# A two-branch layer: w1 blocks paired at a distance, and the rows that their pairing leaves unused no longer loaded

## The chip, the cores and the metric

The kernel runs on one core of a Trainium2 chip. The metric is the device time of one execution in microseconds (us). The kernel before takes 145.11 us, the median of three runs (144.78 to 145.85).

## The reference

The input x has 2048 tokens of D = 448 channels. It is normalised once, and two branches start from the normalised tokens. Both results and x itself are added.

```python
xn = layernorm(A_x)                                # (1, 2048, 448), no scale, no shift
q, k, v = split(xn @ A_wqkv)                       # 16 heads of 28
phi(t) = concat(softmax(t @ w_phi), softmax(-(t @ w_phi)))
o = phi(q) @ (phi(k)^T v) / (phi(q) . sum(phi(k)))  # linear attention
h = silu(xn @ B_w1)                                # 448 -> 1792
out = x + o @ A_wo + h @ B_w2                      # 1792 -> 448
```

Everything is in bf16 with f32 sums. The case is about `B_w1`, the 448 x 1792 matrix of the second branch.

## The kernel before

**The rows of w1.** 448 rows do not fill whole groups of 128 partitions. The kernel holds w1 as four row tiles (kt 0 to 3) that begin at rows 0, 128, 256 and 320 (`KS`). Tile 2 holds rows 256 to 383, tile 3 rows 320 to 447, so rows 320 to 383 are held twice: in the upper half (partitions 64 to 127) of tile 2 and in the lower half of tile 3. `w1_sb` is a view of the buffer `flat` (phT in the profile), 1792 columns per tile; the same buffer later takes the transposed phi(q).

**A pair of column blocks.** w1 has 14 column blocks of 128. `ffn1_block` (L783) multiplies two of them, i = 0 and 1, with 512 tokens, and hands the work to `pair_block` (L755). There block i = 0 uses tile 2 whole and the upper half of tile 3, block i = 1 uses tile 3 whole and the lower half of tile 2. That covers the 448 rows for each, and neither touches the doubled rows of its other tile. Two matmuls of 64 rows run beside each other in the two halves of the array. The pairs fp = 0 to 6 are blocks (0,1), (2,3) and so on. A third function, `evac`, writes Silu of both blocks from PSUM into hT (ScalarE, tile hT).

**The order of the work.** Every operation is recorded once, with its dependencies worked out from the memory that it reads and writes; a list scheduler sets each engine's order, and TensorE's is written out by hand in `PLAN`. Each operation then waits for semaphores of those it depends on. In `PLAN`, aFn and bFn are the first and second half of the matmuls of the n-th pair (n counts the pairs of the first 512 tokens, then those of the next), av and bv, ak and bk, aq and bq the same for two token tiles of v, k and q, f and g the folding of w_phi into wqkv, Y and G the second FFN product, W the output projection. It begins:

```python
PLAN = """r0 aF3@4 r2 r1 bF3 aF6@0 aF4@6 bF6 bF4 aF5@4 av2@2 av0@0 bv2 bF5 bv0 av4@6 aF10@2 ...
```

Before that stands a head in which F0, F1 and F2 (pairs 0, 1, 2 with the first 512 tokens) run token tile by token tile, as the tiles come out of the layernorm, interleaved with TensorE transposes; r0, r1, r2 are their last matmuls, those of the remaining half tiles.

**The loads.** `load` (L561) issues one DMA on SP's queue (three of x go by ScalarE's queue, four small ones by GpSimd's). In order, SP issues: x0; w1_0 (tiles 0 and 1 of columns 0 to 511) and w1_0r (tiles 2 and 3 of them); two loads for columns 512 to 767; x4 (tokens of tiles 4 to 7); two for 768 to 1023; two for 1024 to 1791; two for wv; x8 and x12. `load_rows4` is a load of tiles 0 to 2 and one of tile 3. Behind the loads the same queue issues DMA transposes (`dma_t`, L632): wT_dma4 to 7 (columns of wqkv, for the fold; tiles wT and Y_sb), then xnT_dma5 and xnT_dma7 (the normalised tiles 4 and 5, 6 and 7; xnT<-RA), then wT_dma8 and, with waits for the layernorm, the further ones, then w2 and wo. av4 needs xnT_dma5, aF10 (pair 3 with tokens 512 to 1023) needs xnT_dma7 too, and the first fold, f0, needs wT_dma4 to 8.

Of the kernel before, what the change touches and what calls it, by code (L numbers as in the profile page):

```python
# [8 lines left out]
ACTF = mybir.ActivationFunctionType  # L9
# [361 lines left out]
def bass_parallel_sum__linear_kernel_hedgehog__dense_activation_silu__prompt_kernel(  # L371
# [10 lines left out]
    S, D, H, DH, FF = 2048, 448, 16, 28, 1792  # L382
# [18 lines left out]
    def rows_of(a, t0, t1):  # L401
        for u0, u1 in TILES:
            if u0 <= t0 < u1:
                v = a[0][128 * u0:128 * u1, :].rearrange("(p t) d -> p t d", p=128)
                return v[:, t0 - u0:t1 - u0, :]
# [3 lines left out]
    with es:  # L409
        def sb(name, shape, dt):  # L410
            return es.enter_context(nc.sbuf_tensor(name, shape, dt))
# [26 lines left out]
        hT = sb("hT", [128, FT, S], BF16)  # L438
# [3 lines left out]
        flat = phT[:]  # L442
# [5 lines left out]
        w1_sb = flat[:, 0:4 * FF].rearrange("p (k f) -> p k f", k=4)  # L448
# [59 lines left out]
        def d_mm(n):  # L508
            return max(n * 0.4167 + 2.5, 40.0)

        def d_act(n):
            return n / 1.2 + 60.0
# [7 lines left out]
        def pe_mms(mms, name, dur=None, keys_w=(), mode=128):  # L520
            def fn(e):
                r = None
                for dst, lhsT, rhs, st, sp in mms:
                    r = e.matmul(dst, lhsT, rhs, start=st, stop=sp, skip_group_check=True)  # L524
                return r
            n = 1
            for _, cnt in mms[0][2].ap[1:]:
                n *= cnt
            o = P.op("pe", dur if dur is not None else d_mm(n), fn, reads=[m[1] for m in mms] + [m[2] for m in mms],
                     writes=[m[0] for m in mms], keys_w=keys_w, name=name, mode=mode)  # L530
            o.words = 2 * len(mms)
            return o

        def mm(dst, lhsT, rhs, st, sp, name, keys_w=()):
            pe_mms([(dst, lhsT, rhs, st, sp)], name, keys_w=keys_w)
# [10 lines left out]
        def act(dst, src, func, n, name, scale=1.0, table=None, **keys):  # L546
            P.op("act", d_act(n), lambda e: e.activation(dst, src, func, scale=scale),  # L547
                 reads=[src], writes=[dst], table=table, name=name, **keys)
# [8 lines left out]
        def load(dst, src, name, eng="sp", lat=1700.0):  # L557
            n = 2
            for _, cnt in list(dst.ap):
                n *= cnt  # L560
            P.dma(lambda e: e.dma_start(out=dst, in_=src), n / 280.0, writes=[dst], name=name, eng=eng, lat=lat)  # L561
# [35 lines left out]
        def load_x(t0, t1, eng="sp"):  # L597
            load(x_sb[:, t0:t1, :], rows_of(A_x, t0, t1), f"x{t0}", eng, lat=1400.0)

        def load_rows4(dst, src, c0, c1, name, eng="sp"):  # L600
            load(dst[:, 0:3, :], src[0:KF, c0:c1].rearrange("(k p) f -> p k f", p=128), name, eng)
            load(dst[:, 3, :], src[D - 128:D, c0:c1], name + "r")

        def load_w1(c0, c1, eng="sp"):
            load_rows4(w1_sb[:, :, c0:c1], B_w1, c0, c1, f"w1_{c0}", eng)
# [3 lines left out]
        load_x(2, 3, "act")  # L609
        load_x(3, 4, "act")  # L610
        load(w1_sb[:, 0:2, 0:512], B_w1[0:256, 0:512].rearrange("(k p) f -> p k f", p=128), "w1_0")
        load(w1_sb[:, 2:4, 0:512], bass.AP(B_w1.tensor, B_w1.offset + 256 * FF, [[FF, 128], [64 * FF, 2], [1, 512]]), "w1_0r")
        load_w1(512, 768)
        load_x(4, 8)
        load_w1(768, 1024)
        load_w1(1024, FF)
        load_rows4(wv_sb, A_wqkv, 2 * D, 3 * D, "wv")
        load_x(8, 12)
        load_x(12, 16)
# [135 lines left out]
        def pair_block(b0, width, lhs, rhs, name):  # L755
            def part(c0, c1, steps=(0, 1, 2)):
                for i in range(2):
                    for n, kt in ((n, (0, 1, 2 + i)[n]) for n in steps):
                        mm(banks[b0 + i][:, c0:c1], lhs(i, kt, slice(0, 128)), rhs(i, kt, slice(0, 128), c0, c1),
                           n == 0 and c0 == 0, False, name)  # L760

            def rest():
                rows = [HIGH, LOW]
                return [(banks[b0 + i][:, 0:width], lhs(i, 3 - i, rows[i]), rhs(i, 3 - i, rows[i]), False, True) for i in range(2)]

            first = []

            def half(i):
                lo, hi = i, 1 - i
                mms = []  # L770
                for n, (kl, kh) in enumerate(((0, 0), (1, 1), (2, 3)) if i == 0 else ((0, 0), (1, 1), (2, 2), (3, 3))):
                    st, sp = i == 0 and n == 0, i == 1 and n == 3
                    mms.append((banks[b0 + lo][:, 0:width], lhs(lo, kl, LOW), rhs(lo, kl, LOW), st, sp))
                    mms.append((banks[b0 + hi][:, 0:width], lhs(hi, kh, HIGH), rhs(hi, kh, HIGH), st, sp))
                o = pe_mms(mms, name, dur=len(mms) // 2 * d_mm(width), mode=64)
                if i == 0:
                    first.append(o.id)
                else:
                    o.after = first[0]

            return part, rest, half

        def ffn1_block(fp, c, b0):  # L783
            tok = slice(c * 512, (c + 1) * 512)
            fns = pair_block(b0, 512, lambda i, kt, r: w1_sb[r, kt, (2 * fp + i) * 128:(2 * fp + i + 1) * 128],
                                    lambda i, kt, r, c0=0, c1=512: xnT_sb[r, kt, c * 4 + c0 // 128:c * 4 + c1 // 128, :], "ffn1")

            def evac():
                src = psum[:, b0 * 512:(b0 + 2) * 512].rearrange("p (b c) -> p b c", b=2)
                act(hT[:, 2 * fp:2 * fp + 2, tok], src, ACTF.Silu, 1024, "silu", table="silu", okeys_r=["acttab"])  # L790

            return *fns, evac

# [250 lines left out]
        def F(n, b0):  # L1044
            return ffn1_block(*chunk[n], b0)
# [3 lines left out]
        for word in "tr0a tr0 tr1 00a 10a 00b 10b 01a 11a 01b 11b 20 tr2 21 tr3 02a 12a 22a 02b 12b 22b 03 13 23".split():  # L1049
# [3 lines left out]
            f, t = int(word[0]), int(word[1])  # L1053
# [54 lines left out]
        for word in PLAN.split():  # L1108
            n0 = len(P.ops)
            kind, arg = word[0], word[1:]  # L1110
            if kind == "r":
                b, f = (0, 2, AUX)[int(arg)], head[int(arg)]
                pe_mms(f[1](), "rest", dur=d_mm(512), mode=64)
                f[3]()
            elif kind in "ab":
                turned = kind == "b"
                kind, (arg, _, at) = arg[0], arg[1:].partition("@")
                t = int(arg)
# [12 lines left out]
                elif kind in "GY":  # L1131
                    bs = pair_banks(t, at)
                    k = done.get((t, turned), 0)
# [27 lines left out]
            else:  # L1161
                assert kind == "E"
                t = int(arg)
# [114 lines left out]
```

## Time and profile before

| | |
|---|---|
| median of three runs | 145.11 us |
| the profiled execution | 144.51 us, its span 143.3 us |
| TensorE matmuls (PE) | 140.2 us busy, 98% of the span, granted clock 1.00 |
| VectorE, ScalarE, GpSimd | 90.2, 79.6, 75.2 us busy |
| read from HBM | 6.57 MB |
| loads of w1, as landed | 10.85 and 11.52 us for the last two, 6.3 or less from issue |

The span runs from the first instruction to the end of the last; the profiled execution's own time is 1.2 us more than that. PE counts as busy while a matmul is in its pipeline. Names such as psum<-xnT,phT say what an instruction writes and reads; an L number is a line of the kernel, and since helpers record the operations, all matmuls of the layer have line L524. SPq is the sequencer of SyncE, which issues DMAs; its durations are those of the issue, not of the transfer. A DMA lands when its last packet has been counted.

### The profile page before, as it was taken

The page shows a single profiled execution, that of the slowest core. Times are in us where ns is not written, and L with a number is a line of the kernel's source. Part 1 is how long each engine was busy: PE and PEld are TensorE (multiplying, and loading weights), DVE is VectorE, ACT ScalarE, POOL GpSimd, SP SyncE. Part 2 cuts the span into 40 slices and gives each one's busy share as a digit, 9 for nine tenths or more (in the row PEclk, how much of TensorE's full clock was granted, in tenths as well). Part 3 has the DMA queues.
Part 4 walks back from the last instruction along what each step waited for, and adds up shares of the span by engine and source line. Part 5 has one row for each costly group of instructions (what it writes and reads, how often), then busy time and mean ns, then how long its engine had stood idle before and what let it go on. Part 6 is the DMA issues. An engine that isn't in the chain of part 4 may idle for free.

```text
span 143.3 us, 4555 instructions
## 1 busy us (share of the span) xinstructions
PE 140.2 (98%) x1966; PEld 82.4 (58%) x1966; DVE 90.2 (63%) x194; ACT 79.6 (56%) x98; POOL 75.2 (53%) x95
## 2 busy tenths in 40 slices
PE   7999999999999999999999999999999999999994
PEld 7894444445444544476677655555555555555773
DVE  1988897600850079939049999957976564265533
ACT  4669676479996999888888948265440000000000
POOL 8828566620395009899935999992594800000000
DMA  4999989745990000000000068859589999825522
GB/s 133 354 318 380 165 168 84 158 81 93 344 300 7 0 2 5 0 0 5 0 5 5 5 116 162 129 109 164 97 159 134 230 225 159 143 48 105 167 91 64
DMA packets 45188, 17.59 MB, mean 123 GB/s; under 512 B 36960, under 2 KB 44784, under 8 KB 45168
## 3 DMA queue, kind: packets, MB, share of 16 engines
q1 hardware_dynamic: 42304, 15.14, 54.8%
q10 hardware_dynamic: 2736, 2.14, 5.1%
q8 instruction: 15, 0.25, 0.7%
q0 software_dynamic: 128, 0.03, 0.2%
q14 instruction: 5, 0.04, 0.1%
HBM read 6.57 MB, written 1.84 MB: 59 GB/s over the span
## 4 chain that ended last, share of the span: by engine, by line
PE 95%; DVE 2%; DMA 1%; ACT 0%; issue 0%
PE psum L524 94%; DMA x_sb<-in_A_x_dram 1%; DVE st L709 1%; PE psum L541 1%; DVE RA L724 0%; DVE mv L710 0%; DVE x_sb L1010 0%; ACT ve L713 0%; DVE rstd L715 0%
## 5 line engine op out<-in xcount | busy, mean ns | idle before, releaser
L524 PE MATMUL psum<-xnT,phT 64*128 64x512 bf16 (+1 forms) x428 | 46.8, 350 | 0.0
L524 PE MATMUL psum<-w_sb,hT 64*128 64x448 bf16 (+4 forms) x455 | 46.0, 341 | 0.0
L844 DVE TENSOR_REDUCE Rec<-Ek_sb 128x32 f32<-128x896 bf16 (+1 forms) x20 | 24.6, 1257 | 18.6 <-ACT Ek_sb L547 18.6
L524 PEld LDWEIGHTS psum<-w_sb,hT 64*128 64x128 bf16 (+1 forms) x455 | 23.6, 94 | 17.5 <-issue 0.2
L547 ACT ACTIVATE hT<-psum 128x1024 bf16<-128x1024 f32 x28 | 27.6, 1024 | 10.7 <-PE psum L524 10.6
L524 PEld LDWEIGHTS psum<-xnT,phT 64*128 64x128 bf16 (+1 forms) x428 | 22.4, 95 | 17.7 <-ACT vaug L547 0.7
L881 POOL TENSOR_TENSOR RA<-Ek_sb,Rec 128x896 bf16<-128x896 bf16 x16 | 27.0, 1722 | 6.3 <-DVE Rec L845 4.4
L524 PE MATMUL psum<-Wqk,xnT 64*128 64x432 bf16 x224 | 24.6, 343 | 0.0
L547 ACT ACTIVATE Ek_sb<-psum 128x864 bf16<-128x864 f32 x24 | 20.4, 916 | 7.0 <-PE psum L524 4.1
L854 POOL TENSOR_TENSOR Ek_sb<-Ek_sb,Rec 128x896 bf16<-128x896 bf16 x8 | 13.4, 1696 | 16.4 <-DVE Rec L845 16.4
L524 PEld LDWEIGHTS psum<-Wqk,xnT 64*128 64x128 bf16 x224 | 10.9, 94 | 8.2 <-ACT hT L547 0.4
L547 ACT ACT_TABLE_LOAD x11 | 14.1, 1283 | 2.1 <-POOL Wp L554 1.9
L854 POOL TENSOR_TENSOR phT<-phT,Rec 128x896 bf16<-128x896 bf16 x8 | 13.4, 1697 | 1.2 <-issue 0.9
L524 PE MATMUL psum<-wv,xnT 64*128 64x448 bf16 x112 | 12.4, 349 | 0.0
L709 DVE BATCH_NORM_STATS2 st<-x_sb 128x6 f32<-128x448 bf16 x16 | 9.7, 603 | 3.4 <-DMA x_sb<-in_A_x_dram 3.4
L524 PE MATMUL psum<-wo_sb,vaug 64*128 64x448 bf16 (+2 forms) x102 | 11.3, 338 | 0.0
L1010 DVE TENSOR_TENSOR x_sb<-psum,x_sb 128x448 bf16<-128x448 f32 (+2 forms) x13 | 7.2, 583 | 5.6 <-PE psum L524 5.6
L989 DVE TENSOR_TENSOR vaug<-psum,rden 128x448 bf16<-128x448 f32 x16 | 9.3, 620 | 0.0
L724 DVE TENSOR_SCALAR RA<-x_sb,mv,rstd 128x384 bf16<-128x384 bf16 (+2 forms) x28 | 8.8, 353 | 0.8 <-POOL rstd L720 0.6
L844 DVE TENSOR_REDUCE Rec<-phT 128x64 f32<-128x1792 bf16 x4 | 8.0, 1991 | 1.9 <-ACT phT L547 1.9
L845 DVE RECIPROCAL Rec<-Rec 128x32 f32<-128x32 f32 (+1 forms) x24 | 8.8, 396 | 0.2
L547 ACT ACTIVATE vaug<-psum 128x896 bf16<-128x896 f32 x8 | 7.5, 949 | 2.3 <-PE psum L524 2.3
(60 smaller groups left out, 106.0 us busy)
## 6 DMA issues: line engine op xcount, KB each, us to landing
out_dram<-x_sb ACTq DMA_DIRECT2D x15, 112.0 KB, 2.6
w_sb<-in_B_w_dram SPq DMA_DIRECT2D x1, 1568.0 KB, 7.5
x_sb<-in_A_x_dram SPq DMA_DIRECT2D x3, 448.0 KB, 7.7
wo_sb<-in_A_wo_dram SPq DMA_DIRECT2D x2, 336.0 KB, 7.4
phT<-in_B_w_dram SPq DMA_DIRECT2D x3, 192.0 KB, 4.8
phT<-in_B_w_dram SPq DMA_DIRECT2D x1, 576.0 KB, 6.1
phT<-in_B_w_dram SPq DMA_DIRECT2D x2, 256.0 KB, 3.7
x_sb<-in_A_x_dram ACTq DMA_DIRECT2D x3, 112.0 KB, 3.5
```

The source lines that it names most:

```text
L524: r = e.matmul(dst, lhsT, rhs, start=st, stop=sp, skip_group_check=True)
L541: r = e.transpose(dst, src, ident[:])
L547: P.op("act", d_act(n), lambda e: e.activation(dst, src, func, scale=scale), reads=[src], writes=[dst], table=table, name=name, **keys)
L709: P.op("dve", 590, lambda e: e.bn_stats(st6[:, t, :], xs), reads=[xs], writes=[st6[:, t, :]], name=f"bnst{t}", okeys_w=["ln"])
L724: P.op("dve", dur, lambda e: e.tensor_scalar(dst, x_sb[:, t, c0:c1], mv[:, t, 0:1], rstd[:, t:t + 1], ALU.subtract, ALU.mult), reads=[xs, ...
L844: P.op("dve", 50 + 967 * n, lambda e: e.tensor_reduce(R2, E4, AXL.X, ALU.add), reads=[E4], writes=[R2], name=f"Ssum_{tag}")
L845: P.op("dve", 135 + 210 * n, lambda e: e.reciprocal(R2, R2), reads=[R2], writes=[R2], name="Rrec")
L854: P.op("pool", 1700, lambda e: e.tensor_tensor(E3, E3, Rk[:, :, None].broadcast_to([128, 32, DH]), ALU.mult), reads=[E3, Rk], writes=[E3], ...
L881: P.op("pool", 1700, lambda e: e.tensor_tensor(dst, Eq, Rq.rearrange("p (c j) -> p c j", c=CC)[:, :, :, None].broadcast_to([128, CC, 4, DH ...
L989: P.op("dve", 620, lambda e: e.tensor_tensor(o4, U4[:, :, :, 0:DH], rden4[:, :, :, None].broadcast_to([128, CC, 2, DH]), ALU.mult), reads= ...
L1010: P.op("dve", d_dve(cs.stop - cs.start), lambda e: e.tensor_tensor(res[:, cs], ob, addend[:, cs], ALU.add), reads=[ob, addend[:, cs]], wri ...
```

## The change

The first four column blocks are paired as (0,2) and (1,3) and the last six as (8,11), (9,12), (10,13); blocks 4 to 7 stay paired as neighbours. So within columns 0 to 511 the first 256 columns are always i = 0 and the second 256 always i = 1, and likewise columns 1024 to 1407 and 1408 to 1791.

For such a group, `load_w1_late_rows` loads, in one DMA, tile 2 of the first half of the columns and tile 3 of the second half; `load_w1_rest_rows` loads, in two DMAs of 64 partitions, the upper half of tile 3 of the first columns and the lower half of tile 2 of the second ones. The doubled rows that a pair does not use are left out. For columns 0 to 511 the two rest loads are issued after x4, and r0 is the first to wait for them; for the last six blocks they follow directly. Columns 512 to 1023 are loaded as before. SP's queue gets four more DMAs, ahead of the load of wv; the order of instructions on all other engines stays the same, and r0 and bF6 get a wait for their rest loads.

```diff
-        load(w1_sb[:, 2:4, 0:512], bass.AP(B_w1.tensor, B_w1.offset + 256 * FF, [[FF, 128], [64 * FF, 2], [1, 512]]), "w1_0r")
+
+        def load_w1_late_rows(c, w, name):
+            step = FF + w
+            load(flat[:, 2 * FF + c:2 * FF + c + 2 * step].rearrange("p (k f) -> p k f", k=2)[:, :, 0:w],
+                 bass.AP(B_w1.tensor, B_w1.offset + 256 * FF + c, [[FF, 128], [64 * FF + w, 2], [1, w]]), name)
+
+        def load_w1_rest_rows(c, w, name):
+            load(w1_sb[64:128, 3, c:c + w], B_w1[384:448, c:c + w], name + "s")
+            load(w1_sb[0:64, 2, c + w:c + 2 * w], B_w1[256:320, c + w:c + 2 * w], name + "t")
+
+        load_w1_late_rows(0, 256, "w1_0r")
         load_w1(512, 768)
         load_x(4, 8)
+        load_w1_rest_rows(0, 256, "w1_0")
         load_w1(768, 1024)
-        load_w1(1024, FF)
+        load(w1_sb[:, 0:2, 1024:FF], B_w1[0:256, 1024:FF].rearrange("(k p) f -> p k f", p=128), "w1_1024")
+        load_w1_late_rows(1024, 384, "w1_1024r")
+        load_w1_rest_rows(1024, 384, "w1_1024")
         load_rows4(wv_sb, A_wqkv, 2 * D, 3 * D, "wv")
         load_x(8, 12)
...
         def ffn1_block(fp, c, b0):
             tok = slice(c * 512, (c + 1) * 512)
-            fns = pair_block(b0, 512, lambda i, kt, r: w1_sb[r, kt, (2 * fp + i) * 128:(2 * fp + i + 1) * 128],
+            f0, df = (fp, 2) if fp < 2 else (2 * fp, 1) if fp < 4 else (fp + 4, 3)
+            fns = pair_block(b0, 512, lambda i, kt, r: w1_sb[r, kt, (f0 + df * i) * 128:(f0 + df * i + 1) * 128],
...
-                act(hT[:, 2 * fp:2 * fp + 2, tok], src, ACTF.Silu, 1024, "silu", table="silu", okeys_r=["acttab"])
+                act(hT[:, f0:f0 + df + 1:df, tok], src, ACTF.Silu, 1024, "silu", table="silu", okeys_r=["acttab"])
```

## The prediction

> **What bounds the kernel now.** I read the chain that ended last first, in order of time. Of its 24 pieces these carry the start and the rest:
>
> ```profile
> 0.81 2.13 DMA x_sb<-in_A_x_dram
> ...
> 5.09 0.41 DVE RA L724
> ...
> 5.54 0.40 PE psum L541 x4
> ...
> 8.46 132.82 PE psum L524 x1853
> 141.28 0.02 issue
> ```
>
> The reader is to see that no load of w1 is in it. Up to 5.54 us the chain is the first tile's load and its layernorm; from 8.46 us it is TensorE alone, 132.82 us without a break. Matmul by matmul, the trace has 0.28 us of idle array at 5.54 (the second tile's normalisation), 0.08 at 8.38 and 0.10 at 10.49, and until 138.4 us only one other excess above 0.03 us. So **less traffic has nothing to give back**, except within those 0.3 us or so, none of which follows a load. The question is whether something that TensorE takes in time today comes late.
>
> So next, SP's queue, which issues all these loads and behind them the transposes that TensorE needs (timeline of SP; start, duration; four consecutive pieces first, then a narrow window around single issues):
>
> ```profile
> 1.27 1.98 SPq L561 DMA_DIRECT2D phT<-in_B_w_dram  x4
> 3.29 0.43 SPq L561 DMA_DIRECT2D x_sb<-in_A_x_dram  x1
> 3.77 1.98 SPq L561 DMA_DIRECT2D phT<-in_B_w_dram  x4
> 5.79 1.31 SPq L561 DMA_DIRECT2D wv<-in_A_wqkv_dram  x2
> ...
> 8.38 1.23 SPq L632 DMA_TRANSPOSE wT<-in_A_wqkv_dram  x1
> ...
> 12.29 3.03 SPq L632 DMA_TRANSPOSE Y_sb<-in_A_wqkv_dram  x1
> 15.37 1.31 SPq L632 DMA_TRANSPOSE xnT<-RA  x1
> 16.72 1.33 SPq L632 DMA_TRANSPOSE xnT<-RA  x1
> 18.09 1.27 SPq L632 DMA_TRANSPOSE Y_sb<-in_A_wqkv_dram  x1
> ```
>
> SP issues without a pause from 0.81 to 19.4 us. One issue stands out: the fourth weight transpose (wT_dma7) holds SP for 3.03 us, its three sisters for 1.23 to 1.30. Behind it come the two transposes of tiles 4 to 7 (xnT_dma5, xnT_dma7), then wT_dma8. By the DMA view of narrow windows they land 3.3, 3.2 and 3.2 us after their issue starts: at 18.70, 19.95 and 21.33 us. Their users, in the timeline of PE:
>
> ```profile
> 19.09 1.49 PE L524 MATMUL psum<-wv,xnT 64*128 64x448 bf16 x14
> 20.41 0.81 PE L524 MATMUL psum<-xnT,phT 64*128 64x512 bf16 x6
> ...
> 23.32 0.19 PE L524 MATMUL psum<-BD,wT 64*128 64x56 bf16 x1
> ```
>
> The first row is bv0 (8 matmuls) and av4, which starts at 19.84 and needs xnT_dma5: 1.14 us of slack. The second is aF10, which needs xnT_dma7: **0.46 us, the thinnest cover near the change**. The third is the fold, which needs wT_dma8: 1.99 us.
>
> Last, why the 3.03 us: busy time by windows (the last three columns are granted clock, DMA share, GB/s).
>
> ```profile
> 13.50:14.00 0.50, 0.50 (x8) 0.24 (x6) 0.28 (x1) 0.50 (x2) 0.50 (x2) 1.00 0.93 323
> 14.00:14.50 0.50, 0.50 (x8) 0.25 (x6) 0.48 (x2) 0.50 (x1) 0.39 (x2) 1.00 4.60 217
> 14.50:15.00 0.50, 0.50 (x8) 0.20 (x4) 0.12 (x1) 0.20 (x1) 0.00 (x0) 1.00 1.56 49
> 15.00:15.50 0.50, 0.50 (x8) 0.23 (x6) 0.50 (x1) 0.47 (x1) 0.00 (x0) 1.00 0.05 22
> 15.50:16.00 0.50, 0.50 (x8) 0.26 (x6) 0.47 (x3) 0.50 (x2) 0.19 (x1) 1.00 0.42 91
> ```
>
> The DMA queue nearly stands still from 14.5 to 15.5 us: packets of the transposes that should take 18 ns stay open for 1.1 to 1.75 us, while single 3584-byte packets of the last x load trickle through until 15.35. A 16,384-byte packet of the instruction queue ran at 12.02 us for 1.08 us. I read it as one DMA engine late by that packet, the transposes waiting for it, and SP held because its queue is full; SP is let go at 15.32, when the trickle ends.
>
> **The change, part by part.**
> - *Bytes.* First group 512 to 448 KB, last six blocks 768 to 672 KB: 160 KB less. The trace's packets take 27 ns (512 B), 47 (1024), 70 (1536), 41 (896). First group: 256 packets at 47 become 384 at 27, over 16 engines 0.75 to 0.65 us. Last: 512 at 70 become 256 at 70 and 384 of 768 B, estimated at 36 between the neighbours, 2.24 to 1.98 us. Sum: the queue is **0.36 us shorter** from the wv load on.
> - *Issues.* Four more on SP (two of 32 KB, two of 48 KB), all ahead of wv. Four loads and their gaps take 2.02 us (1.27 to 3.29), so 0.505 each; the 64-row load of wor took 0.59 and 0.05 gap at 37.66. Four: **+2.02 us**, bounds 1.8 to 2.6. (The other wor issue took 1.64 behind a busy queue; none of the 13 early issues exceeds 0.76.)
> - *SP after.* wT_dma7 starts at 12.29 + 2.02 = 14.31 and, being let go at 15.32 or a little sooner, needs only its own 1.27: it ends at 15.58. So 1.76 of the 2.02 us fall into the hold, and xnT_dma5 and 7 are issued **0.26 us later**; bounds 1.8 and 2.6 give 0.04 and 0.84. xnT_dma7 lands at 20.21 (19.99 to 20.79) for 20.41. A landing is taken up within about 0.05 us (x0 landed 2.94, first statistics 2.96). Stall **0**, bounds 0 and 0.43. wT_dma8 lands at 21.6 (to 22.2) for 23.32, covered; the other xnT transposes and wT_dma0 to 3 land over 4.5 us before their users, w2 11 us.
> - *New wait of r0.* r0 (10.49 us) now also waits for the two rest loads, issued after x4. They should land with it, near 8 us (x4 at 7.81, 128 packets more); as slow as the slowest 64 KB load (5.5 us from issue) it is 9.8. Behind r0 in TensorE's queue stands everything; cover 0.7 us at worst, cost 0.
> - *w1 columns 768 to 1023* landed at 9.71 for aF3 at 10.72; 0.1 us less queue ahead, but issue 1.0 later: 9.6 to 10.7, cost 0 to 0.05. Column blocks 8 to 13: 11.52 for aF6 at 12.66; the rows that aF6 needs come sooner, the rest is for bF6 at 13.96. Cost 0.
> - *Pairing.* The matmuls of every engine's order stay the same in number, shape and place; the two blocks of a pair are only other columns, and the Silu writes hT with a stride between its two 512-column runs. Cost 0; nothing in the trace bounds the stride, at 28 Silus of 1.02 us with 10.6 us of waiting for PE I take none.
>
> **Sum:** 144.51 us (span 143.3) plus 0, up to +0.5, down to -0.3. The profiled run is 0.6 below the median of 145.11, so about 145.1 to 145.2 in the median.
>
> A rule of the Trainium skill speaks against the small loads. "DMA: Bandwidth & Descriptors", Rules for kernel authors, advises one 128-partition transfer over two halves, and says that below 64 KB one pays mostly overhead; its fixed 2 us each, paid in series, would be an estimated 8 us, and with it a stall of some 7.6 us and about 152.7 us. The 64 KB load of this trace landed 0.19 us after the 192 KB one ahead (6.44 to 6.63), so by this case's rows such a cost is overlapped.
>
> **The rivals.**
> - *The hold moves with the issues* (slower). If wT_dma7 is held 3.03 us wherever it stands, nothing is absorbed: xnT_dma7 lands 1.8 to 2.6 us later, 21.8 to 22.6, and aF10 waits 1.4 to 2.2 us. It decides from a shift of 0.41 us on. Time 146.5 to 147.3 in the median; if the next standstill (22.5 to 23.5 us, 2 and 9 GB/s) catches the transposes too, 1.3 more. For it: the cause is inferred. Against: the release coincides with the end of the trickle, and the issue at 30.29 (2.03 us) is long beside the next 16 KB packet (30.31). The Trainium skill, "Runtime: NRT & Kernel Launch", Instruction fetch mechanics, calls the cost of such a fetch mostly hidden; by that rule the hold would have another cause, and this rival's time would follow. The trace's standstills at 14.5 and 22.5 us follow such packets.
> - *Each small load costs the queue what the slowest did*: 1.12 us between landings (8.59 to 9.71), four times, less 0.36: 4.1 us late, aF10 stalls 3.7, 148.8. Against it, the queue was full (302 to 359 GB/s) in that time.
> - *Faster*: an earlier landing lifts the start. The idle before 10.5 us is 0.5 in all; 144.6.
>
> **How the numbers follow.** A measurement of this kernel tells about 1% from no change. Forecast 0.80, moved hold 0.13, slow small loads 0.02, faster 0.05 (nearly all of it under 1%). The range goes from 144.3 to 147.0, into the moved hold; the forecast's own is 144.4 to 145.8. Faster by over 1%: 0.03; slower: 0.14; same: 0.83.
>
> **What would show it.** Right: wT_dma7 takes about 1.3 us instead of 3.03 and ends near 15.5; xnT_dma7 lands at 20.0 to 20.4; PE keeps 132 to 133 us without a break; the last x load lands some 0.3 us sooner than 15.99. Wrong: a hole in PE at 20.4 us (moved hold), before 10.7 (rest loads late), or at 23.3 (wT_dma8 caught by the second standstill).

## The result, and the profile after

The changed kernel takes 145.68 us, the median of 22 runs (144.68 to 146.17); the kernel before took 145.00 us beside it, also of 22 (144.52 to 145.85). The ratio is **1.0035, 95% interval 1.002 to 1.005**: slower by about 0.5 us by the ratio (the medians differ by 0.68), clear of noise with so many runs and a third of the 1% that the prediction took as the least that a measurement can tell.

The profiled execution took 144.68 us, its span 143.4. It is the fastest of the 22, so it is likely to show less of the loss than the others. Its chain that ended last (start, duration, what):

```profile
0.85 4.00 PE psum L591 x36
...
8.46 12.11 PE psum L524 x132
20.57 0.04 issue
20.61 120.88 PE psum L524 x1722
141.49 0.02 issue
```

The 132.82 us of TensorE without a break are now two pieces. The cut lies at 20.57 us, at aF10, the place with the thinnest cover. SP's queue, in the timeline (start, duration):

```profile
3.76 4.51 SPq L561 DMA_DIRECT2D phT<-in_B_w_dram  x8
8.31 1.12 SPq L561 DMA_DIRECT2D wv<-in_A_wqkv_dram  x2
9.47 0.91 SPq L561 DMA_DIRECT2D x_sb<-in_A_x_dram  x2
10.42 1.61 SPq L645 DMA_TRANSPOSE wT<-in_A_wqkv_dram  x1
12.08 3.84 SPq L645 DMA_TRANSPOSE Y_sb<-in_A_wqkv_dram  x3
15.96 2.69 SPq L645 DMA_TRANSPOSE xnT<-RA  x2
18.69 1.26 SPq L645 DMA_TRANSPOSE Y_sb<-in_A_wqkv_dram  x1
```

wT_dma4 starts at 10.42 instead of 8.38, 2.04 us later. The long hold of wT_dma7 is gone (three transposes in 3.84 us, 1.28 each), but now wT_dma4 is the one that takes longer, 1.61 us. xnT_dma5 is issued at 15.96, 0.59 later than before, and xnT_dma7 lands 3.2 us after its issue start of 17.32, at 20.48. PE's rows:

```profile
19.09 1.49 PE L524 MATMUL psum<-wv,xnT 64*128 64x448 bf16 x14
20.61 0.82 PE L524 MATMUL psum<-xnT,phT 64*128 64x512 bf16 x6
```

aF10 starts at 20.61 instead of 20.41. That 0.20 us is the one new hole of this execution. The others of the first 11 us are as before within 0.1 us, and the rest loads, w1's columns 768 to 1023 and the fold are in time.

### The profile page after: what moved, and what is told of

It reads as the page before. It is cut to its first block, busy times and chain, and to the rows that moved or that the text cites. A ratio compares the mean times of both kernels' runs of the same rounds, so it can differ in the third digit from the quotient of the medians.

```text
span 143.4 us, 4564 instructions
## 1 busy us (share of the span) xinstructions
PE 140.6 (98%) x1966; PEld 82.9 (58%) x1966; DVE 90.3 (63%) x194; ACT 79.6 (56%) x98; POOL 75.2 (52%) x95
## 4 chain that ended last, share of the span: by engine, by line
PE 98%; DVE 0%; issue 0%
PE psum L524 94%; PE psum L591 3%; PE psum L541 1%; DVE x_sb L1024 0%
## 5 line engine op out<-in xcount | busy, mean ns | idle before, releaser
L547 ACT ACTIVATE hT<-psum 128x1024 bf16<-128x1024 f32 x28 | 27.6, 1023 | 10.7 <-PE psum L524 10.7
L547 ACT ACTIVATE Ek_sb<-psum 128x864 bf16<-128x864 f32 x24 | 20.4, 916 | 6.2 <-PE psum L524 4.3
```

## The experiments

Four causes were set against each other. **A**: the four added issues on SP make xnT_dma5 and xnT_dma7 late, and aF10 waits. **B**: loads of half height slow the DMA queue by themselves. **C**: the new pairing or the stride of the Silu's writes. **D**: the fold's transposes are caught by the second standstill of the DMA queue, the one that the prediction saw at 22.5 to 23.5 us. When neither A nor B fitted the first runs, a fifth came up, **E**, below. A transpose is called held when its issue takes longer than the usual 1.2 to 1.3 us. Ratios are to the kernel before on the same chip.

### The pairing alone

```diff
+            f0, df = (fp, 2) if fp < 2 else (2 * fp, 1) if fp < 4 else (fp + 4, 3)
...
-                act(hT[:, 2 * fp:2 * fp + 2, tok], src, ACTF.Silu, ...
+                act(hT[:, f0:f0 + df + 1:df, tok], src, ACTF.Silu, ...
```

> The new pairing of the column blocks with the loads of the kernel before (all rows loaded, no load added). Theory A (four more DMA issues on SP make xnT_dma5 and 7 late, and aF10 waits): ratio to the kernel before 1.000, within 0.15%, no hole in PE at 20.4 us, xnT_dma7 landing near 19.95. Rival C (the pairing itself, the stride of the Silu's writes): the whole 1.0035 of the change.

144.78 us against 144.97, ratio 0.9986 (0.9975 to 0.9996). C falls: the pairing and the stride cost nothing. In its profile xnT_dma7 landed at 20.58, not near 19.95, and aF10 waited 0.11 us.

### The first four blocks alone, the last six alone

```diff
-        load(w1_sb[:, 0:2, 1024:FF], ...)
-        load_w1_late_rows(1024, 384, "w1_1024r")
-        load_w1_rest_rows(1024, 384, "w1_1024")
+        load_w1(1024, FF)
```

That is the first; the second keeps the loads of columns 0 to 511 as they were and changes those of 1024 to 1791. In each, the blocks whose loads are not changed are paired as neighbours, as before.

> The change for the first four column blocks alone: two more issues on SP, some 1.0 us, 64 KB less. Theory A with a hold of SP that swallows the first 1.76 us: ratio 1.000 to 1.001, xnT_dma7 lands at 19.9 to 20.3, no hole or one under 0.05 us at aF10. A without such a hold (every issue counts): half of the change's loss, 1.0017. Rival B (the half-height loads slow the DMA queue): about half as well.

1.0003 (0.9984 to 1.0021). In its profile xnT_dma5 was issued at 15.26, earlier than in the kernel before, and yet xnT_dma7 landed at 20.62 and aF10 waited 0.39 us; at most 20.3 and 0.05 had been expected.

> The change for the last six column blocks alone: two more issues, 96 KB less, two half-height loads of 48 KB ahead of wv. By itself the first group gave 1.0003. If the loss sits in the last group's loads: ratio 1.002 to 1.005. If it needs both groups (the issues add up): 1.000, within 0.15%.

1.0006 (0.998 to 1.0032). Neither half shows a loss. But half of the change's loss would be 0.17%, and both intervals have room for that, so these two runs do not tell a threshold from a loss in proportion. The profile of the second (145.74 us, one of its slower runs) has a hole of 0.57 us at aF10: wT_dma4 started at 9.80 and got through, but SP was held on wT_dma6 and wT_dma7, and xnT_dma5 was issued only at 16.34. A further 0.69 us went ahead of bv0.

### Four issues more, no other change

```diff
-        load_w1(768, 1024)
-        load_w1(1024, FF)
+        for k in range(3):
+            load(w1_sb[:, k, 768:1024], B_w1[128 * k:128 * k + 128, 768:1024], f"w1_768_{k}")
+        load(w1_sb[:, 3, 768:1024], ...)
...
```

The loads of columns 1024 to 1791 are split in the same way.

> The kernel before, with its loads of tiles 0 to 2 of w1 columns 768 to 1023 and 1024 to 1791 issued tile by tile: four more issues on SP, some 2.0 us, with the same packets in the same order and no half-height load. Theory A: like the change, ratio 1.002 to 1.005, wT_dma4 issued near 10.4, xnT_dma7 landing 20.2 to 20.8 and a hole in PE at 20.4 us of up to 0.4. Rival B (half-height loads and their packets slow the queue): 1.000, xnT_dma7 near 20.0. Rival C: 1.000.

0.9996 (0.9982 to 1.0009). **A misses in its plain form**: four issues more, and no loss on average. But they took less than those of the change: wT_dma4 starts at 9.69 here, 0.73 us earlier than in the changed kernel. SP:

```profile
9.69 1.21 SPq L636 DMA_TRANSPOSE wT<-in_A_wqkv_dram  x1
10.94 1.99 SPq L636 DMA_TRANSPOSE Y_sb<-in_A_wqkv_dram  x1
```

The hold falls on the second transpose, wT_dma5, and xnT_dma5 is issued at 15.58. A loss in proportion to the delay of wT_dma4 (1.31 us of the change's 2.04) would be 0.22%, more than the interval allows; this run is what speaks for a threshold. Its profile is the slowest of its 12 runs (145.70 us), with a hole of 0.34 us at the fold and one of 0.4 us at 136 us.

### The changed kernel with the tile transposes one place earlier

```diff
-        chain("x8 x12 wT_dma4 wT_dma5 wT_dma6 wT_dma7 xnT_dma5 xnT_dma7 wT_dma8 ...
+        chain("x8 x12 wT_dma4 wT_dma5 wT_dma6 xnT_dma5 xnT_dma7 wT_dma7 wT_dma8 ...
```

> The changed kernel with xnT_dma5 and xnT_dma7 issued one place earlier on SP, ahead of wT_dma7. Theory A: both land some 1.3 us sooner (xnT_dma7 near 19.2), no hole at 20.4; wT_dma7 lands 2.7 us later, near 20.7, still ahead of the fold at 23.3: ratio to the kernel before 0.997 to 1.001. Rival B where the queue and not SP is late: xnT_dma7 lands less than 0.5 us sooner and the loss stays in part. Rival C: 1.0035.

1.0038 (1.0019 to 1.0057): a miss in the time, and informative in the trace. PE's timeline:

```profile
20.84 0.82 PE L524 MATMUL psum<-xnT,phT 64*128 64x512 bf16 x6
21.48 0.94 PE L524 MATMUL psum<-wv,xnT 64*128 64x448 bf16 x8
22.24 1.69 PE L524 MATMUL psum<-xnT,phT 64*128 64x512 bf16 x14
24.85 0.18 PE L524 MATMUL psum<-BD,Y_sb 64*128 64x56 bf16 x1 [0.92 <-DMA Y_sb<-in_A_wqkv_dram]
```

aF10 loses 0.11 us, but the fold starts 1.08 us after its predecessors have gone through (14 matmuls from 22.24 are seven pairs at 0.216, to 23.77), waiting for a weight transpose. The loss moved two blocks on. The transpose waited for is wT_dma8. It was issued at 19.91 instead of 18.09, but it landed at 24.71, 4.80 us after its issue, where the kernel before had 3.25. At 3.25 it would have been there at 23.2, ahead of the fold. So SP's lateness alone does not make this hole: issued later, the transpose met the standstill that D speaks of (46 and 19 GB/s from 23 to 24 us).

### The changed kernel, two more profiled executions

> The changed kernel once more, for a second profiled execution: the first one was its fastest of 22. Theory D (in a usual execution the second standstill of the DMA queue, after the instruction packet near 22 us, catches wT_dma8 and the fold waits): time 145.3 to 146.2, wT_dma8 landing after 23, a hole in PE of 0.3 to 1.1 us at 23.5 to 25. Theory A (aF10 alone): a hole of 0.4 to 1.0 at 20.4 to 21 and none at the fold.

> The same, a third profiled execution. D: a hole at the fold in this one or the other; A: at aF10 alone in both.

They took 145.95 and 146.07 us, both above the median of 145.68. The first of the two, SP and then PE:

```profile
10.41 2.41 SPq L645 DMA_TRANSPOSE wT<-in_A_wqkv_dram  x1
12.87 3.85 SPq L645 DMA_TRANSPOSE Y_sb<-in_A_wqkv_dram  x3
16.76 2.68 SPq L645 DMA_TRANSPOSE xnT<-RA  x2
```

```profile
19.23 0.92 PE L524 MATMUL psum<-wv,xnT 64*128 64x448 bf16 x8
20.32 0.74 PE L524 MATMUL psum<-wv,xnT 64*128 64x448 bf16 x6 [0.17 <-DMA xnT<-RA]
21.89 0.82 PE L524 MATMUL psum<-xnT,phT 64*128 64x512 bf16 x6 [0.82 <-DMA xnT<-RA]
```

D falls for the changed kernel: there is no hole at the fold in either. The holes are at av4 and aF10, named with their releaser. av4's 8 predecessors take four pairs of 0.189 us, so av4 could have started at 19.99 and aF10 0.57 us after av4: 0.33 and 1.00 us lost, 1.3 in all (0.12 and 1.02 in the third execution). SP shows the larger part of the reason. The issue of wT_dma4 takes 2.41 us, to 12.82. From there three further weight transposes have to be issued ahead of xnT_dma5, 3.9 us with their gaps; nothing holds SP any more, and nothing is left to absorb. xnT_dma5 starts at 16.76 and xnT_dma7 at 18.11, both 1.39 us later than before.

The rest is not SP's. xnT_dma7 lands at 21.75, 1.80 us later than before: 0.41 us of that is a longer way from issue to landing, 3.64 us instead of 3.23. In the third execution the two parts are 1.32 and 0.57 us. Neither A to D nor E, which follows, speaks of this second part. (bv0 had started 0.14 and 0.41 us late already, ahead of all this; in the second profile of the kernel before it is 0.26.)

**E**: what matters is on which transpose SP is held, since every transpose left to issue after the release puts xnT_dma5 off by 1.3 us. After a hold on wT_dma7 none is left, after one on wT_dma4 three are. In the change wT_dma4 starts at 10.42 and is caught; in the profiles where it started at 9.8 or earlier it got through. Getting through is not enough by itself: in the profile of the last six blocks the two last weight transposes were held instead, to 16.29.

### The rest loads at full height

```diff
-            load(w1_sb[64:128, 3, c:c + w], B_w1[384:448, c:c + w], name + "s")
-            load(w1_sb[0:64, 2, c + w:c + 2 * w], B_w1[256:320, c + w:c + 2 * w], name + "t")
+            load(w1_sb[:, 3, c:c + w], B_w1[320:448, c:c + w], name + "s")
+            load(w1_sb[:, 2, c + w:c + 2 * w], B_w1[256:384, c + w:c + 2 * w], name + "t")
```

> The changed kernel with its four rest loads at full height (128 partitions, 160 KB more, as many bytes as before the change; the rows added are not used). As many issues as in the change. Theory B (half-height loads slow the queue): ratio to the kernel before 1.000 to 1.002. If the issues or the new place of the loads cost: 1.003 to 1.005 or more, since the queue is not shorter any more.

0.9998 (0.9972 to 1.0024). The same number of issues and 160 KB more than the change, and no loss shows (one of 0.24% would still fit). SP:

```profile
3.75 3.89 SPq L561 DMA_DIRECT2D phT<-in_B_w_dram  x8
7.68 0.97 SPq L561 DMA_DIRECT2D wv<-in_A_wqkv_dram  x2
8.69 0.92 SPq L561 DMA_DIRECT2D x_sb<-in_A_x_dram  x2
9.65 1.22 SPq L645 DMA_TRANSPOSE wT<-in_A_wqkv_dram  x1
10.92 1.93 SPq L645 DMA_TRANSPOSE Y_sb<-in_A_wqkv_dram  x1
```

The eight w1 loads take 3.89 us of SP instead of 4.51. One half-height issue takes 0.48 to 0.60 us in the changed kernel, the same four at full height 0.43 to 0.47; the load behind each pair of them is shorter too (0.44 instead of 0.59 us). wT_dma4 starts at 9.65, gets through in 1.22, and the hold falls on wT_dma5. This fits B as well as E, so the next run had to part them.

### Six issues more, all at full height

The split of four above, and wv split in the same way.

> The kernel before with three loads issued tile by tile (w1 columns 768 to 1023, 1024 to 1791, and wv): six more issues of about 0.47 us, all at full height, the same packets and bytes. Theory E: wT_dma4 starts near 10.6, as late as in the changed kernel, is held to about 12.8, xnT_dma5 is issued at 16.5 or later, a hole of 0.6 to 1.4 us at av4 and aF10, ratio to the kernel before 1.003 to 1.008. Theory B (half-height loads in themselves): 1.000, within 0.15%.

145.95 us against 144.95, **1.0056 (1.0033 to 1.0079)**. E predicted it, B did not: no half-height load, the packets and bytes of the kernel before, and a loss no smaller than the change's (the intervals overlap). SP and PE:

```profile
10.42 2.19 SPq L638 DMA_TRANSPOSE wT<-in_A_wqkv_dram  x1
12.66 3.85 SPq L638 DMA_TRANSPOSE Y_sb<-in_A_wqkv_dram  x3
16.55 2.68 SPq L638 DMA_TRANSPOSE xnT<-RA  x2
```

```profile
22.33 0.82 PE L524 MATMUL psum<-xnT,phT 64*128 64x512 bf16 x6 [1.56 <-DMA xnT<-RA]
```

wT_dma4 starts at 10.42 as in the change, is held to 12.62, and aF10 waits. Set beside the run before it this is the clearest case of E: the release comes at 12.85 there and at 12.62 here, but there two transposes are left and xnT_dma5 is issued at 15.49, here three and it is 16.55. The hole at aF10 is 1.72 us and the one at av4 0.08, more than the 0.6 to 1.4 that E expected. xnT_dma7 landed 2.24 us later than in the kernel before, 1.18 by its issue and 1.06 by the way to its landing (4.29 us). So E has about half of that lateness.

### The kernel before, once more

> The kernel before once more, for a second profiled execution. Theory E (in the changed kernel SP is held at the first weight transpose, wT_dma4, which leaves three others to be issued after it and ahead of xnT_dma5; in the kernel before the hold falls on the third or fourth): SP held at wT_dma6 or wT_dma7, xnT_dma5 issued before 16.0, holes at aF10 below 0.4 us.

144.78 us, no hole at av4, aF10 or the fold. SP:

```profile
8.12 1.22 SPq L632 DMA_TRANSPOSE wT<-in_A_wqkv_dram  x1
...
12.17 3.22 SPq L632 DMA_TRANSPOSE Y_sb<-in_A_wqkv_dram  x1
15.44 2.68 SPq L632 DMA_TRANSPOSE xnT<-RA  x2
```

The hold is on wT_dma7 again, and ends at 15.39 (15.32 in the first profile).

### The kernel before with the tile transposes one place earlier

The edit of the chain above, in the kernel before.

> The kernel before with xnT_dma5 and xnT_dma7 one place earlier on SP, ahead of wT_dma7. If its usual executions lose time at aF10 only: ratio 0.997 to 0.999, no hole at 20.4. If the fold is next in line, as in the changed kernel with this order (its fold waited 1.08 us): a hole at 23.3 to 25 and 1.000 to 1.004.

1.0017 (0.9998 to 1.0036), a hole of 0.31 us at the fold and none at aF10: wT_dma8 landed 4.71 us after its issue at 18.89. No gain is shown, so nothing speaks for this order.

### The changed kernel with two rest loads on ScalarE's queue

```diff
-            load(w1_sb[0:64, 2, ...], name + "t")
+            load(w1_sb[0:64, 2, ...], name + "t", "act")
...
-        chain("x1 x2 warm_act x3 ve0 ve1 ev0a ev0 ev1a ev1 ve2 ve3 ev2a ...
+        chain("x1 x2 warm_act x3 ve0 ve1 w1_0t ev0a ev0 ev1a ev1 ve2 ve3 w1_1024t ev2a ...
```

> The changed kernel, all its loads and bytes kept, with one rest load of each group (w1_0t and w1_1024t) issued by ScalarE's queue between its layernorm steps instead of SP's: two issues less on SP, about 1.2 us. Theory E: wT_dma4 is issued near 9.2 to 9.3, escapes the hold near 12.8, which falls on wT_dma5 or later; xnT_dma5 is issued before 16.0 and xnT_dma7 lands before 20.8; hole at aF10 at most 0.45; ratio to the kernel before 0.998 to 1.002. Theory B (half-height loads in themselves): still 1.003 to 1.004, with holes of 1 us at av4 and aF10. A cost on ScalarE would show as a later transposed tile at 5.5 or 8.4 us.

144.82 us against 145.18, 0.9988 (0.9965 to 1.001). SP and PE:

```profile
9.30 1.42 SPq L645 DMA_TRANSPOSE wT<-in_A_wqkv_dram  x1
10.77 4.63 SPq L645 DMA_TRANSPOSE Y_sb<-in_A_wqkv_dram  x3
15.44 2.78 SPq L645 DMA_TRANSPOSE xnT<-RA  x2
```

```profile
20.74 0.82 PE L524 MATMUL psum<-xnT,phT 64*128 64x512 bf16 x6 [0.17 <-DMA xnT<-RA]
```

All loads and bytes of the change are there, half height included; only 1.1 us of issuing have left SP. xnT_dma5 is back at 15.44 and the loss is gone. With the run of six issues, this shows on the changed kernel itself that the loss is issue time on SP; that it acts through the place of the hold is read from the profiles. This execution still has a hole of 0.33 us at aF10: xnT_dma7 landed at 20.61, 3.7 us after its issue. Holes of 0.39 stand in the profiles of the first four blocks alone and of the full-height loads too, whose ratios are 1.000. In these three the issue is within 0.16 us of the kernel before, so the holes come from the way to the landing (3.73 to 3.92 us). One profile is one draw, and only the ratios carry the mean. No kernel of these beats the one before by more than its interval, but for the pairing alone, by 0.14%, whose cause was not looked for.

## Why the prediction was right, and where it was not

The time was held (145.1 to 145.2 forecast, 145.68 measured, 144.3 to 147.0 given), and so was "within 1%". That is in part luck: the step that was to absorb the added issues failed, and what its failure cost was small. In the profiles the loss comes from that step and, for a smaller part, from a second one, the landing.

- *What bounds the kernel; nothing to gain.* Right. TensorE runs without a break but for the new hole. The bytes saved did not even come out as a shorter queue: the last x load landed at 16.26 us, where 15.99 less 0.36 was expected. The packets took longer (512-byte packets 33 ns on average instead of 28, 896-byte ones 49 instead of 43), and the sum of the packets' times from 2 to 13.5 us, shared over 16 engines, is 12.2 us instead of 12.1.
- *Four issues, 2.02 us.* wT_dma4 came 2.04 us later, but the match is luck. The four issues with their gaps took 2.40 us, not 2.02, and the loads around them 0.35 us less than in the profile that was read. With the same loads wT_dma4 started at 8.38, 8.12 and 7.86 (the kernel before twice and the pairing alone). At full height, with four more issues too, it started at 9.65; the half height made the other 0.77 us.
- **"1.76 of the 2.02 us fall into the hold"** is the step that failed. It took the hold for a date, 15.32 us, that SP meets wherever it stands. In the changed kernel SP is held earlier, on wT_dma4, and let go at 12.03, 12.82 and 12.76 us in three executions; after that 3.9 us of issuing are left. xnT_dma5 was issued 0.59, 1.39 and 1.32 us later, not 0.26, and the stall was 0.20, 1.3 and 1.1 us, not 0. The reading behind the date was loose as well: the last packet of the x loads ended at 15.51, so SP was let go 0.19 us before the trickle was over, not when it ended.
- *The landing.* The prediction carried over 3.2 us from the issue of xnT_dma7 to its landing. It was 3.16, 3.64 and 3.80 us in the three executions, and up to 0.57 us of the stall is this term.
- *The moved hold*, the rival with 0.13. Nearer in its mechanism: the hold went with the queue, and was not absorbed. But it is not wT_dma7's 3.03 us in another place; it is 0.4 to 1.2 us on another transpose, and its price of 1.4 to 2.2 us was too high. Its test, "a hole in PE at 20.4 us", came out.
- *A page of the Trainium skill was set against the change*: "DMA: Bandwidth & Descriptors", Rules for kernel authors, one 128-partition transfer rather than two halves. I weighed it by bytes and overlap, where the trace was against it. The runs bear on it by another way than the one that the page gives, the shared engines, and without joining two halves into one: at full height the same four loads leave SP 0.77 us earlier, and no loss shows.
- *r0, columns 768 to 1023, the fold, the stride.* Right: the rest loads landed at 8.29 and 8.83 us for 10.49, the columns at 9.75 for 10.72, and the pairing alone costs nothing.

Two things stay open. Why SP is held where it is was seen, not taken apart: no run moved the instruction packets by themselves. And no run was made on why xnT_dma7 takes 3.2 us to its landing in some executions and 3.6 to 4.3 in others.

## What to carry to other kernels

Where TensorE is full, fewer bytes gain nothing, and a load can cost the time of its issue on a queue that also issues what TensorE waits for. Here that price had a threshold: four quick issues more showed no loss, four slow ones cost 0.35% and six quick ones 0.56%. In the profiles, SP's stall had moved in the latter two from the last of a series of transposes to the first. A stall that seems to end at a fixed time may move with the work ahead of it; that should be tested before anything is booked against it, and with losses this small one profile is not enough; here the first one was the fastest execution of 22.

## What the runs showed of the hardware

- SP took 0.48 to 0.60 us to issue a load of 64 partitions (the changed kernel) and 0.43 to 0.47 for one of 128 in the same four places, with twice the bytes (the rest loads at full height).
- In ten of the fourteen profiles the held transpose was let go 0.41 to 0.44 or 1.04 to 1.06 us after a 16,384-byte packet of the instruction queue had ended (after it 10.54 + 1.08 = 11.62 and 12.03 in the changed kernel's first profile, 10.47 + 1.29 = 11.76 and 12.82 in its second). The kernel before (twice), the pairing alone and the kernel before with the turned order are the other four; there SP was let go only at 15.32 to 16.19 us, 0.19 us before the last packet of the x loads ended in three of them and 0.57 us after it in the turned order. The Trainium skill, "Runtime: NRT & Kernel Launch", Instruction fetch mechanics, has the cost of such a fetch mostly hidden. The coincidence here does not refute that: it does not show that the packet is the cause.
- The packet started at 10.43 to 10.54 us in four profiles with the changed kernel's loads on SP, at 12.02 and 12.08 in the kernel before and between 11.11 and 12.99 in the other eight, with TensorE at the same work. Why was not tried.
- xnT_dma7 landed 3.2 to 3.3 us after its issue in the kernel before (twice), the pairing alone and the changed kernel's first profile, and 3.6 to 4.3 us in its other two, in both splits, in either group alone, at full height and with ScalarE's queue. wT_dma8 took 3.0 to 3.3 us in the kernel before, and 5.60, 4.80 and 4.71 us where the fold waited (four issues more, and the two turned orders). The cause was not looked for.
